# A 128-byte pad that moves the weight tiles of an attention and two-MLP kernel to 256-byte addresses

## The chip, the cores and the metric

One core of a Trainium2 chip runs the whole program. The metric is the device time of one execution in microseconds (us); the median of several executions counts. The profile shows one execution of the same program, recorded instruction by instruction. PE is the matrix engine, PEld its weight load, DVE, ACT and POOL are the other compute engines, and SP issues most of the transfers.

## The reference

```python
# attention: 2 batches, 8 heads, 768 positions, head dimension 64
scores = q @ k.T / 8 + bias          # bias: distance times a slope per head
scores = where(keep, scores, -1e9)   # keep: 8 global keys, 96 local ones
a = exp(scores - max); a = a / (sum(a) + 1e-9)
x = (a @ v) as (1536, 512)
# first block, d_ff 2048
h = x @ w_in;  g = h * sigmoid(h);  x = g @ w_out
# second block, d_ff 1536
g = sigmoid(x @ w_gate) * (x @ w_val);  out = g @ w_out2
```

All inputs and the output are float32 (the weights arrive in a wider layout of two words and are rebuilt on the chip).

## The kernel before

Every large product is done in three passes over pairs of fp32r tiles: each operand is split into a high part and a low part, and hi*hi, hi*lo and lo*hi are added in PSUM. So every activation tile and every weight tile holds two planes: `X[g]` is `[128, 2, 4, 512]` (lines 75, 512), `g` tiles are `[128, 2, 512]` (lines 519 and 533), weight tiles `W[n]` are `[128, 2, 512]` (lines 78 and 920).

The work has two stages. First comes attention with the first half of the first block woven between its steps (`att_units`, `macro`, `window`): there PE alternates between short runs of attention products, PE transposes against `ident`, and fp32r products. Then comes `phase_rest` (line 630), with nothing but fp32r products left for PE: `H(ti)` makes 12 products (24 in the second block) that read an `X` tile and one or two weight tiles into a PSUM bank; `Y(ti)` makes 12 products that read one `g` tile and one weight tile. The order is written out: an `H` run, then the `Y` run of an earlier task, and so on over 68 tasks. Each product of these is 128x128 stationary by 128x512 moving.

- `mm3` (line 501, product on line 503) serves the `H` runs: weight slice stationary, `X` slice moving ("bank<-x,w"). In the attention stage it also serves the output half (`y_part`, line 578): weight slice stationary, `g` slice moving ("bank<-g,w" on L503), in runs of 3 per output slice.
- Line 680 is `Y` of the first block: weight stationary, `g` moving. Line 682 is `Y` of the second: `g` stationary, weight moving.

Weight tiles are filled by `dma_w` (transfer into a `stage` tile), `to_f32` and `split_w` (lines 151 to 168, on ACT and DVE), paced by `pump_w`.

Tiles are laid in the SBUF in the order in which pools and tiles are made. In the program before, byte addresses within a partition are these (they are the compiled program's own):

| tiles | first address | remainder by 256 | by 512 |
|---|---|---|---|
| `ident` | 16512 | 128 | 128 |
| `X[0]`, `X[1]`, `X[2]` | 17152, 33536, 49920 | 0 | 256 |
| `acc[0]`, `acc[1]` | 66304, 74496 | 0 | 256 |
| `nm_all` (384 bytes) | 82688 | 0 | 256 |
| `W[0]` to `W[15]`, every 4096 | 83072 ... | 128 | 128 |
| `stage`, `u`, `g`, `sg` tiles | 148608 ... | 128 | 128 |
| `acc2`, `W[16]` to `W[23]` (made after attention) | 185472, 193664 ... | 128 | 128 |
| attention's `mask`, `kt` | 185472 ... | 128 | 128 |
| attention's `qk`, `v`, `t`, `pt` | 196576 ... | 224 | 480 |

The slices that a product reads start at multiples of 512 bytes within a tile (stationary) or of 1024 (moving), so a slice has its tile's remainder.

Of the kernel before, what the change touches and what calls it, by code (L numbers as in the profile page):

```python
# [8 lines left out]
F32 = mybir.dt.float32  # L9
# [23 lines left out]
def attn_moe_moe2_kernel(  # L33
# [14 lines left out]
    nc = tc.nc  # L48
# [15 lines left out]
    main = fast.enter_context(tc.tile_pool(name="main", bufs=1))  # L64
# [10 lines left out]
    X = [main.tile([128, 2, KD, G], F32R, name=f"x{g}") for g in range(NG)]  # L75
    acc = [main.tile([128, 4, 512], F32, name=f"acc{g}") for g in range(2)]
    nm_all = main.tile([128, NBLK, H], F32, name="nm_all")
    W = [main.tile([128, 2, 512], F32R, name=f"w{n}") for n in range(16)]


# [60 lines left out]
    def wtile(key):  # L141
        return W[wid[key] % 24]

    def slot_free(n):
        if n < 16:
            return True
        if n < 24:
            return len(W) == 24
        return wfree[n - 24] >= 0
# [13 lines left out]
    def split_w(n):  # L163
        w = W[n % 24]
        st = u_p.tile([128, 512], F32, tag="u", name="u")
        to_f32(st, stages.pop(n))
        nc.scalar.activation(out=w[:, 0, :], in_=st, func=AF.Copy)  # L167
        nc.vector.tensor_tensor(w[:, 1, :], st, w[:, 0, :].bitcast(F32), ALU.subtract)  # L168
# [728 lines left out]
    with ExitStack():  # L897
# [21 lines left out]
        for n in range(16, 24):  # L919
            W.append(late.tile([128, 2, 512], F32R, name=f"w{n}"))  # L920
        wst["gap"] = 7
# [38 lines left out]
```

## Time and profile before

| | us |
|---|---|
| median of 3 runs | 691.22 (691.2 to 691.92) |
| the profiled execution, first to last instruction | 690.8 |
| PE busy in it | 676.4 (98%) |
| DVE, ACT, POOL busy | 374.2, 277.5, 84.6 |

The profiled execution's span lies 0.4 us below the median; what lies around the span in a timed run is about that. A matmul's duration in the profile is from its start to its modelled end, with its passage through the pipeline; successive matmuls overlap. So the pace of PE is read from starts: in a merged row of n matmuls, (length of the row minus one matmul's mean duration) / (n - 1) is the mean distance from one start to the next.

### The profile page before, as it was taken

What the parts mean: (1) busy time and instruction counts of PE and PEld (TensorE: products, weight loads), DVE (VectorE), ACT (ScalarE), POOL (GpSimd) and SP (SyncE); (2) the same over time, 40 slices, a digit from 0 to 9 for tenths busy, and PEclk for the clock granted to TensorE, in tenths of its full rate; (3) what the DMA queues carried; (4) which work ended last, traced back from release to release, by engine and by line L of the source; (5) the groups of instructions that cost most, each with busy time, mean ns of one, the idle gap of its engine ahead of it and who ended that gap; (6) DMA issues with size and microseconds to landing.
All of it is one profiled execution on the core that took longest, in us unless ns stands there. A gap on an engine that the chain in (4) does not pass through costs nothing.

```text
span 690.8 us, 9290 instructions
## 1 busy us (share of the span) xinstructions
PE 676.4 (98%) x3463; PEld 539.7 (78%) x3463; DVE 374.2 (54%) x869; ACT 277.5 (40%) x594; POOL 84.6 (12%) x166
## 2 busy tenths in 40 slices
PE   9999999999999999999999999999999999999995
PEld 7567886777778888888888888888888888888884
DVE  4999976534659999452499831211882311212112
ACT  3887865554645555332456521111451111111110
POOL 4255563342410000000000000000000000000000
PEclk9999999999999999999999999999999999999998
DMA  9766652210005554300025420000240000100101
GB/s 212 172 168 170 169 139 62 64 29 3 17 6 155 158 172 136 108 1 0 31 82 169 136 71 1 0 1 0 85 130 0 1 0 1 61 1 23 39 1 65
DMA packets 65301, 49.05 MB, mean 71 GB/s; under 512 B 39648, under 2 KB 60128, under 8 KB 65248
## 3 DMA queue, kind: packets, MB, share of 16 engines
q1 hardware_dynamic: 64032, 48.11, 24.7%
q8 instruction: 29, 0.48, 0.3%
q10 hardware_dynamic: 1216, 0.26, 0.2%
q14 instruction: 24, 0.20, 0.1%
HBM read 45.22 MB, written 3.15 MB: 70 GB/s over the span
## 4 chain that ended last, share of the span: by engine, by line
PE 94%; DVE 4%; issue 1%; ACT 0%; DVEq 0%
PE bank L503 54%; PE bank L682 14%; PE bank L680 13%; PE bank L377 4%; PE bank L449 3%; PE bank L428 2%; PE bank L895 2%; PE bank L340 1%; DVE t L392 1%; DVE acc L589 1%; DVE u L156 0%; DVE w L168 0%; DVE acc L701 0%; DVE ssum L405 0%; DVE u L159 0%
## 5 line engine op out<-in xcount | busy, mean ns | idle before, releaser
L503 PE MATMUL bank<-x,w 128*128 128x512 f32 (+1 forms) x1488 | 354.9, 389 | 0.0
L503 PEld LDWEIGHTS bank<-x,w 128*128 128x128 f32 x1488 | 272.6, 188 | 61.3 <-issue 0.8
L540 DVE TENSOR_TENSOR sg<-sg,bank 128x512 f32<-128x512 f32 x36 | 24.8, 688 | 167.7 <-PE bank L503 167.7
L682 PE MATMUL bank<-w,g 128*128 128x512 f32 x432 | 104.5, 390 | 0.0
L682 PEld LDWEIGHTS bank<-w,g 128*128 128x128 f32 x432 | 81.1, 188 | 17.8
L680 PE MATMUL bank<-g,w 128*128 128x512 f32 x384 | 93.0, 390 | 0.0
L680 PEld LDWEIGHTS bank<-g,w 128*128 128x128 f32 x384 | 72.1, 188 | 16.0
L537 ACT ACTIVATE sg<-bank 128x512 f32<-128x512 f32 x36 | 21.5, 597 | 120.5 <-PE bank L503 120.4
L541 ACT ACTIVATE g<-sg 128x512 fp32r<-128x512 f32 x36 | 22.8, 633 | 93.5 <-DVE sg L540 93.5
L503 PE MATMUL bank<-g,w 128*128 128x512 f32 (+1 forms) x240 | 54.0, 360 | 2.6 <-DVE acc L589 1.3
L154 ACT ACTIVATE u<-stage 128x512 f32<-128x512 f32 x68 | 45.7, 675 | 26.6 <-DVE w L168 26.1
L411 POOL TENSOR_SCALAR t<-t,ssum 128x256 f32<-128x256 f32 (+1 forms) x88 | 48.8, 569 | 61.4 <-DVE ssum L406 23.0
L168 DVE TENSOR_TENSOR w<-u,w 128x512 fp32r<-128x512 f32 x68 | 47.0, 693 | 12.0 <-ACT w L167 11.9
L167 ACT ACTIVATE w<-u 128x512 fp32r<-128x512 f32 x68 | 42.5, 629 | 26.6 <-PE bank L503 10.8
L399 ACT ACTIVATE t<-t,nm_all 128x256 f32<-128x256 f32 (+1 forms) x96 | 46.1, 484 | 17.0 <-DVE nm_all L392 17.0
L159 DVE SCALAR_TENSOR_TENSOR u<-stage,u 128x512 int32<-128x512 int32 x68 | 48.2, 709 | 0.3
L156 DVE SCALAR_TENSOR_TENSOR u<-stage,u 128x512 int32<-128x512 int32 x68 | 46.9, 689 | 0.6
L503 PEld LDWEIGHTS bank<-g,w 128*128 128x128 f32 x240 | 38.0, 189 | 10.6 <-DVE acc L589 3.8
L392 DVE CUSTOM_DVE_ANT_0 t<-bank,mask 128x256 f32<-128x256 f32 (+1 forms) x96 | 33.7, 396 | 17.6 <-PE bank L377 16.7
L528 ACT ACTIVATE g<-sg 128x512 fp32r<-128x512 f32 x48 | 30.3, 631 | 22.4 <-DVE sg L527 11.9
L527 DVE SCALAR_TENSOR_TENSOR sg<-sg,bank 128x512 f32<-128x512 f32 x32 | 21.9, 684 | 30.0 <-ACT sg L526 29.9
L526 ACT ACTIVATE sg<-bank 128x512 f32<-128x512 f32 x32 | 19.1, 596 | 42.9 <-PE bank L503 42.6
(90 smaller groups left out, 515.3 us busy)
## 6 DMA issues: line engine op xcount, KB each, us to landing
stage<-in_moe_w_out_dram SPq DMA_DIRECT2D x28, 512.0 KB, 3.6
stage<-in_moe_w_in_dram SPq DMA_DIRECT2D x16, 512.0 KB, 3.7
stage<-in_moe_w_gate_dram SPq DMA_DIRECT2D x12, 512.0 KB, 3.6
stage<-in_moe_w_val_dram SPq DMA_DIRECT2D x12, 512.0 KB, 3.5
v<-in_v_dram SPq DMA_DIRECT2D x12, 256.0 KB, 3.6
out_dram<-acc SPq DMA_DIRECT2D x12, 256.0 KB, 2.0
qk<-in_k_dram SPq DMA_DIRECT2D x11, 256.0 KB, 3.6
qk<-in_q_dram SPq DMA_DIRECT2D x11, 256.0 KB, 3.9
```

The costliest lines, as they stand in the source:

```text
L154: nc.scalar.activation(out=st, in_=hw.bitcast(F32), func=AF.Copy, scale=2.0 ** -112)
L156: nc.vector.scalar_tensor_tensor(out=ui, in0=lw, scalar=29, in1=ui, op0=ALU.logical_shift_right, op1=ALU.bitwise_or)
L159: nc.vector.scalar_tensor_tensor(out=ui, in0=hw, scalar=-2 ** 31, in1=ui, op0=ALU.bitwise_and, op1=ALU.bitwise_or)
L167: nc.scalar.activation(out=w[:, 0, :], in_=st, func=AF.Copy)
L168: nc.vector.tensor_tensor(w[:, 1, :], st, w[:, 0, :].bitcast(F32), ALU.subtract)
L392: nc.vector.tensor_tensor_reduce(t[:, e, 0:w], sp[e], mask[e][:, m0:m0 + w], op0=ALU.add, op1=ALU.min, scale=-c, scalar=3.0e38, accum_out= ...
L399: nc.scalar.activation(out=t[:, e, 0:w], in_=t[:, e, 0:w], func=AF.Exp, scale=-1.0, bias=nm_all[:, gi, 2 * p + e:2 * p + e + 1], accum_out ...
L411: nc.gpsimd.tensor_scalar(t[:, e, 0:w], t[:, e, 0:w], ss[:, e:e + 1], 1.0, op0=ALU.mult, op1=ALU.mult)
L503: nc.tensor.matmul(ps, wl[(slice(None), a) + wsl], xl[(slice(None), b) + xsl], start=(first and j == 0), stop=(last and j == len(order) - 1),)
L528: nc.scalar.activation(out=gt[:, 0, :], in_=sg, func=AF.Copy)
L680: nc.tensor.matmul(yb[d], w[:, a, sl], gt[:, b, :], start=st, stop=en)
L682: nc.tensor.matmul(yb[d], gt[:, a, sl], w[:, b, :], start=st, stop=en)
```

## The change

A tile of 32 float32 per partition, 128 bytes, is allocated between `nm_all` and `W`, and GpSimd writes zeros into it once. Every tile allocated behind it lies 128 bytes higher: the weight, `stage`, `u`, `g` and `sg` tiles, `acc2` and `mask`/`kt` then have remainder 0 by 256 (256 by 512, as `X` has), and `qk`, `v`, `t`, `pt` have remainder 96 by 256. `ident`, `X`, `acc` and `nm_all` stay.

```diff
     X = [main.tile([128, 2, KD, G], F32R, name=f"x{g}") for g in range(NG)]
     acc = [main.tile([128, 4, 512], F32, name=f"acc{g}") for g in range(2)]
     nm_all = main.tile([128, NBLK, H], F32, name="nm_all")
+    pad = main.tile([128, 32], F32, name="pad")
+    nc.gpsimd.memset(pad, 0.0)
     W = [main.tile([128, 2, 512], F32R, name=f"w{n}") for n in range(16)]
```

## Rows read from the trace of the kernel before

**Rows 1.** Page: span, busy time, granted clock, chain that ended last by engine
```profile
span 690.8 us, 9290 instructions
PE 676.4 (98%) x3463; PEld 539.7 (78%) x3463; DVE 374.2 (54%) x869; ACT 277.5 (40%) x594; POOL 84.6 (12%) x166
PEclk9999999999999999999999999999999999999998
PE 94%; DVE 4%; issue 1%; ACT 0%; DVEq 0%
```

**Rows 2.** Busy time by stretch: length, then each engine (instructions), clock, DMA
```profile
core 0: us, PE busy (x) PEld busy (x) DVE busy (x) ACT busy (x) POOL busy (x), PEclk, DMA share, GB/s
112.00:200.30 88.30, 86.92 (x575) 65.15 (x571) 44.32 (x157) 45.11 (x123) 30.46 (x61) 1.00 0.12 25
200.30:400.00 199.70, 199.70 (x868) 162.68 (x867) 150.71 (x260) 99.02 (x163) 0.00 (x0) 1.00 0.33 102
400.00:682.80 282.80, 282.77 (x1223) 229.18 (x1221) 85.38 (x135) 55.28 (x90) 0.00 (x0) 1.00 0.07 24
```

**Rows 3.** Groups by shape, 200.3 us to end: busy us, mean ns, idle before
```profile
L503 PE MATMUL bank<-x,w 128*128 128x512 f32 x1248 | 302.4, 395 | 0.0
L503 PEld LDWEIGHTS bank<-x,w 128*128 128x128 f32 x1248 | 234.3, 188 | 55.4
L682 PE MATMUL bank<-w,g 128*128 128x512 f32 x432 | 104.5, 390 | 0.0
L680 PE MATMUL bank<-g,w 128*128 128x512 f32 x384 | 93.0, 390 | 0.0
...
L167 ACT ACTIVATE w<-u 128x512 fp32r<-128x512 f32 x52 | 32.5, 630 | 25.1 <-PE bank L503 10.8 <-DVE u L159 8.0 <-PE bank L682 4.0
...
L503 PE MATMUL bank<-g,w 128*128 128x512 f32 x24 | 6.3, 397 | 0.0
```

**Rows 4.** Timeline of PE, end of attention (start us, length us), then the last runs
```profile
199.27 1.09 PE L449 MATMUL bank<-pt,v 128*64 128x128 f32 x16
200.29 1.66 PE L503 MATMUL bank<-g,w 128*128 128x512 f32 x6
201.79 5.73 PE L503 MATMUL bank<-x,w 128*128 128x512 f32 x24
207.36 1.55 PE L503 MATMUL bank<-g,w 128*128 128x512 f32 x6
...
674.43 8.34 PE L682 MATMUL bank<-w,g 128*128 128x512 f32 x36
```

**Rows 5.** Timeline of PE inside the last H run and the last Y run
```profile
664.63 9.96 PE L503 MATMUL bank<-x,w 128*128 128x512 f32 x42
...
676.26 6.51 PE L682 MATMUL bank<-w,g 128*128 128x512 f32 x28
```

**Rows 6.** Chain that ended last, in order of time: start us, length, what
```profile
446.90 5.59 PE bank L503 x24
452.49 2.73 PE bank L682 x12
```

**Rows 7.** Timeline of PE inside runs of 256 moving columns, attention stage
```profile
65.31 1.36 PE L503 MATMUL bank<-g,w 128*128 128x256 f32 x10
...
72.41 2.69 PE L503 MATMUL bank<-x,w 128*128 128x256 f32 x21
```

**Rows 8.** Groups by shape, 0 to 200.3 us, PE
```profile
L503 PE MATMUL bank<-x,w 128*128 128x512 f32 x144 | 37.7, 401 | 0.0
L503 PE MATMUL bank<-g,w 128*128 128x512 f32 x121 | 33.6, 408 | 1.7 <-DVE acc L589 1.3
...
L428 PE MATMUL bank<-ident,t 128*128 128x128 f32 x176 | 28.3, 280 | 0.0
...
L340 PE MATMUL bank<-ident,qk 128*128 128x128 f32 x96 | 20.4, 288 | 1.1 <-ACT kt L353 0.7 <-DVE kt L351 0.4
...
L503 PE MATMUL bank<-x,w 128*128 128x256 f32 x96 | 14.8, 295 | 0.0
L503 PE MATMUL bank<-g,w 128*128 128x256 f32 x96 | 14.7, 292 | 0.9 <-DVE acc L587 0.9
```

**Rows 9.** Timeline of the first 7 us: what GpSimd makes and who needs it
```profile
0.72 0.20 POOL masks.py:197 MEMSET ident<- 128x128 f32 x1 [0.29 <-POOLq L942]
...
1.53 0.29 POOL masks.py:199 TENSOR_SCALAR_AFFINE_SELECT ident<-ident 128x128 f32<-128x128 f32 x1
1.61 0.43 DVE L251 CAST t<-t 128x384 f32<-128x384 int32 x1 [0.62 <-POOL t L249]
...
4.86 0.17 DVE L230 CAST nf<-nraw 128x4 f32<-128x4 int32 x1 [2.82 <-DMA nraw<-in_n_local_dram]
...
6.80 0.27 PE L340 MATMUL bank<-ident,qk 128*128 128x128 f32 x1
```

**Rows 10.** The end of the chain that ended last
```profile
681.45 1.89 DVE acc L701 x3
683.34 0.29 DVEq L925
683.64 0.29 DVE acc L701
```

## The prediction, made before the change was run

> **What bounds the kernel now.** I read the page first, then the busy time by stretch, then single runs of matmuls on PE's timeline. PE is busy for 676.4 of 690.8 us and makes 94% of the chain that ended last, at a granted clock of 0.9 or more in every slice, the last one apart [rows 1]. From 200.3 us on, when attention is over, PE is busy in 199.70 of 199.70 us and then in 282.77 of 282.80 us at a clock of 1.00 [rows 2], and no matmul group there has any idle time before it [rows 3]. DVE is busy for 150.71 us of the first of these stretches and 85.38 us of the second [rows 2], and a step of the weight preparation (L167) waits for PE, not PE for it [rows 3]. So in the last 482 us only one thing can change the time: the distance from one matmul's start to the next.
>
> **The pace of PE there.** The stage holds 1248 + 432 + 384 + 24 = 2088 products of 512 columns [rows 3]. The first starts at 200.29, the last ends at 674.43 + 8.34 = 682.77 [rows 4]; without the last one's own 0.39 us that is 482.09 us for 2087 distances, 231.0 ns each. But the distances are not alike. Inside the last H run (L503, X moving, weight stationary) it is (9.96 - 0.395) / 41 = 233.3 ns; inside the last Y run (L682) it is (6.51 - 0.39) / 27 = 226.7 ns [rows 3, 5]. Both are 128x128 by 128x512 at the same clock, with one weight load for each product, with nothing to wait for. In the middle of the stage it is the same: an H piece of the chain takes 5.59 / 24 = 232.9 ns each, a Y piece 2.73 / 12 = 227.5 [rows 6]. (A Y run comes in a little slower and then settles: 12 x 227.5 = 2730, less nine at 226.7, leaves 230 ns for each of its first three.) The last Y run goes over three tasks, thus over three pairs of weight and g tiles, and L682 has g stationary and the weight moving while L680 has it the other way round; both groups have the same mean of 390 ns against 395 for L503 [rows 3]. So neither a new tile nor the roles of the tiles make the difference.
>
> What does differ is where the operands start. In Y both start at remainder 128 by 512. In H the weight slice starts at 128 and the X slice at 256. The start of the slice within a tile can't matter much: H steps through four slices of each weight plane and of each X plane, and the mean stays. I take this as the reason: the load of the next product's weights (188 ns, with no time of its own on PE's path [rows 3]) reads the SBUF while the present product streams its moving operand, and the two lie better or worse to each other by the distance of their start addresses.
>
> **The change part by part.**
> *The addresses.* X stays at 256 by 512; weight and g tiles go from 128 to 256. H gets the distance 0 that Y has now; Y keeps its distance of 0. If distance alone decides, each of the 2087 distances becomes 226.7 ns, those at the entrance of a Y run too, since there is no other pace to come from: 2087 x 226.7 = 473.1 us in place of 482.1, a gain of 9.0 us. About 1248 x (232.8 - 226.7) = 7.6 us of it comes from H, the rest from the first products of Y runs and from 24 products of L503 on g. If the entrance of Y stays as it is, the gain is 7.6: that is the lower bound of this case.
>
> *The attention stage.* The 144 products of X there have a mean of 401 ns, the 121 on g, whose operands are at distance 0 already, 408 [rows 8]. They come in short runs between attention's work; six on g take (1.55 - 0.397) / 5 = 230.6 ns each, and the 24 on X beside them (5.73 - 0.395) / 23 = 232.0 [rows 4]. Runs too short to settle gain little, so I count nothing there; the upper bound is some 200 products by 5 ns, 1.0 us. Products of 256 columns show next to no difference: (2.69 - 0.295) / 20 = 119.8 ns on X, (1.36 - 0.292) / 9 = 118.7 on g [rows 7, 8]. I count nothing for them. PE's transposes read `ident` (which stays at 128) and tiles that go from 224 to 96. No row shows that pair of remainders. Bounded by the nearest effect, 6.6 ns either way on 176 + 96 transposes [rows 8], that is 1.8 us up or down; I take 0, since their distance is no more a multiple of 256 after than before.
>
> *The memset.* The nearest row is the memset of `ident` on the same engine, 0.20 us for four times the columns [rows 9]. It may push GpSimd's first work back by up to that. What covers it: `ident` is ready at 1.82 us and PE first uses it at 6.80; the positions that DVE casts at 1.61 us are followed by a wait of 2.82 us for a transfer [rows 9]. Cost 0; without that cover, 0.2 us. GpSimd does nothing after 200.3 us [rows 2]. The order of instructions comes from a planner that simulates times, so one instruction more can exchange neighbours elsewhere in attention: I leave 0.3 us either way for that.
>
> *The others.* ACT's and DVE's operands move by 128 bytes too. They are not on the path before the last evacuation; the tail is three additions of 1.89 us together, one more of 0.29, and the last transfer [rows 10]; I count no change.
>
> Sum: 690.8 - 9.0 = 681.8 us of span, and with the 0.4 us between span and median 691.2 - 9.0 = 682.2. What is late next is still PE: with 231.0 going to 226.7 it asks for weights 2% earlier, and DVE, at 150.71 of 199.70 us, has a quarter to spare.
>
> **The rivals.**
> *It doesn't matter (691.2 us).* The cause could be something else in which H differs from Y: X's two planes lie 8 KiB apart, those of g and W 2 KiB, and H steps to a new X slice every three products. For it: the trace has no run of 512 columns on X at distance 0. Against it: Y's pace didn't change when it stepped to other tiles. The price is that of the whole effect, so the time stays. [...]
>
> *A moving operand at remainder 0 by 256 is itself the slow one (695 us).* H's moving operand starts there and is slow, Y's starts at 128 and is fast [rows 5]; the trace can't tell that from distance, since it has only these two pairs. Then H stays as it is, and all 816 Y products and the 24 on g take H's 232.8 ns in place of 228.1 on average: 840 x 4.7 = 3.9 us more, 695.1. The place is lines 680 and 682; it decides as soon as a settled Y run goes over 230 ns. Against it: a cost of a single stream's start should show as well at 256 columns, where it is within 1.1 ns [rows 7], though there the weight load of 188 ns [rows 3] may hide either cause.
>
> **How the numbers follow.** Forecast (distance decides): 0.64. No effect: 0.19. Slower by the moving start or by the unknown pairs: 0.17. Predicted time 682.2. Its own range is 680.6 (attention gains its 1.0 us, planner 0.3, transposes a little) to 685.5 (entrance of Y runs stays, 1.4, and 1.8 us lost on transposes). The whole range must take in the case of no effect, with the 0.4 us by which the slowest run of before stands off: 680.5 to 691.9. A measurement of this kernel tells about 0.2% (1.4 us) from no change; by that, faster 0.64, same 0.19, slower 0.17.
>
> **What would show it.** Right: in the last H run 42 matmuls in 0.395 + 41 x 0.2267 = 9.69 us in place of 9.96, H pieces of the chain at 5.44 us for 24, the mean of L503 on X in the last stage at 390 ns, Y groups still at 390 or just under, and the attention stage's end within 0.5 us of 200.3. The second rival would show as Y pieces of 2.8 us for 12. No effect would show as 9.96 again. I am wrong if the pace goes to a third value on all groups, or if transposes change by more than 6 ns each.

## The result and the profile after

The kernel with the pad takes 681.88 us (median of 4 runs, 681.57 to 682.99) against 691.57 us (4 runs, 691.20 to 692.33). The ratio on record is 0.9866, with a 95% interval of 0.9852 to 0.988; the quotient of the two medians is 0.9860. The forecast was 682.2. Over all runs of the kernel before that were taken beside the experiments, 19 of them, its median is 691.26. Line numbers of the kernel after are larger by 2.

The page of the kernel after, the lines that answer to [rows 1] (PEclk is the granted clock in 40 slices of the span, in tenths):

```profile
span 680.0 us, 9291 instructions
PE 667.6 (98%) x3463; PEld 540.1 (79%) x3463; DVE 374.2 (55%) x869; ACT 277.9 (41%) x594; POOL 84.6 (12%) x167
PEclk9899999999999999999999999999999999999999
PE 93%; DVE 5%; ACT 1%; issue 0%; DVEq 0%
```

PE's busy time is 8.8 us less; that of no other engine has changed by more than 0.4 us. The 8 in the clock's row lies in the attention stage: from 27 to 34 us the granted clock was 0.76 on average, and from 29 to 32 us it was 0.50; the trace before has 1.00 from 27 to 34 us. PE had been busy for 12.00 of the 12 us ahead of it, as in the trace before. The last stage doesn't see it. Busy time by stretch (length, then each engine with its instructions, granted clock, DMA share, GB/s), as in [rows 2]:

```profile
112.00:199.60 87.60, 86.22 (x570) 64.99 (x568) 44.06 (x155) 45.09 (x123) 30.07 (x60) 1.00 0.11 24
199.60:400.00 200.40, 200.40 (x886) 165.94 (x885) 152.40 (x263) 100.49 (x164) 0.00 (x0) 1.00 0.34 105
400.00:672.90 272.90, 272.90 (x1206) 225.88 (x1204) 83.11 (x131) 54.37 (x88) 0.00 (x0) 1.00 0.07 22
```

PE has no gap in the last stage, as before, and the clock is 1.00 as before; in about the same 200 us it makes 886 products in place of 868. So the pace is what changed. The groups by shape from 199 us on (busy us, mean ns, idle before), to be read beside [rows 3]:

```profile
L505 PE MATMUL bank<-x,w 128*128 128x512 f32 x1248 | 294.7, 389 | 0.0
L505 PEld LDWEIGHTS bank<-x,w 128*128 128x128 f32 x1248 | 234.2, 188 | 48.6
L684 PE MATMUL bank<-w,g 128*128 128x512 f32 x432 | 103.9, 389 | 0.0
L682 PE MATMUL bank<-g,w 128*128 128x512 f32 x384 | 92.4, 389 | 0.0
```

The products on X have lost their 395 ns and stand at 389 with the others; the weight load's 188 ns is what it was. The timeline of PE (start us, length us) gives the stage's two ends, and the insides of the last H run and the last Y run, for [rows 4] and [rows 5]:

```profile
199.61 1.66 PE L505 MATMUL bank<-g,w 128*128 128x512 f32 x6
...
664.87 8.32 PE L684 MATMUL bank<-w,g 128*128 128x512 f32 x36
```

```profile
655.80 8.55 PE L505 MATMUL bank<-x,w 128*128 128x512 f32 x37
...
666.68 6.51 PE L684 MATMUL bank<-w,g 128*128 128x512 f32 x28
```

H: (8.55 - 0.389) / 36 = 226.7 ns, where it was 233.3. Y: 6.51 us for 28, to the digit what it was. The stage lasts from 199.61 to 664.87 + 8.32 = 673.19, 473.58 us in place of 482.48: 8.9 us less. In the chain that ended last (start us, length, what), where [rows 6] had 5.59 and 2.73:

```profile
441.99 5.44 PE bank L505 x24
447.43 2.72 PE bank L684 x12
```

12 x 226.7 = 2.72: the slow entrance of the Y runs is gone too. Taken over all starts in the trace, the distance is 226.67 ns on average for the 1248 products on X, for L682 and for L684 alike; on X it was 232.8 and for L680 and L682 of the kernel before 228.2 and 228.0.

The span fell by 10.8 us, 1.9 more than the stage. That rest isn't the change's. 0.7 us of it lies ahead of 200 us, where the first product on loaded data starts 0.9 us earlier (6.80 us in [rows 9]):

```profile
5.91 0.27 PE L342 MATMUL bank<-ident,qk 128*128 128x128 f32 x1
```

In the experiments below it starts between 5.5 and 7.0 us, with no relation to the pads. The other 1.2 us lie behind the last product: 8.0 us from its end to the span's end before, 6.8 after. In experiment 1 below, which has the same pace, that stretch is 8.2 us; it varies by itself. The timed difference from the 691.26 of the 19 runs, 9.4 us, has less of it.

### The profile page after: what moved, and what is told of

Its sections match the earlier page's. It is cut to its first block, busy times and chain, and to the rows that moved or that the text cites. A ratio compares the mean times of both kernels' runs of the same rounds, so it can differ in the third digit from the quotient of the medians.

```text
span 680.0 us, 9291 instructions
## 1 busy us (share of the span) xinstructions
PE 667.6 (98%) x3463; PEld 540.1 (79%) x3463; DVE 374.2 (55%) x869; ACT 277.9 (41%) x594; POOL 84.6 (12%) x167
## 4 chain that ended last, share of the span: by engine, by line
PE 93%; DVE 5%; ACT 1%; issue 0%; DVEq 0%
PE bank L505 54%; PE bank L684 14%; PE bank L682 13%; PE bank L379 4%; PE bank L451 3%; PE bank L430 2%; PE bank L897 2%; PE bank L342 1%; DVE t L394 1%; DVE acc L591 1%; DVE w L170 0%; DVE u L158 0%; DVE u L161 0%; DVE acc L703 0%; ACT t L401 0%
## 5 line engine op out<-in xcount | busy, mean ns | idle before, releaser
L505 PE MATMUL bank<-x,w 128*128 128x512 f32 (+1 forms) x1488 | 347.1, 384 | 0.0
L684 PE MATMUL bank<-w,g 128*128 128x512 f32 x432 | 103.9, 389 | 0.0
L684 PEld LDWEIGHTS bank<-w,g 128*128 128x128 f32 x432 | 81.1, 188 | 16.8
L682 PE MATMUL bank<-g,w 128*128 128x512 f32 x384 | 92.4, 389 | 0.0
L682 PEld LDWEIGHTS bank<-g,w 128*128 128x128 f32 x384 | 72.1, 188 | 15.0
```

Source lines behind the costliest of these rows:

```text
L505: nc.tensor.matmul(ps, wl[(slice(None), a) + wsl], xl[(slice(None), b) + xsl], start=(first and j == 0), stop=(last and j == len(order) - 1),)
L682: nc.tensor.matmul(yb[d], w[:, a, sl], gt[:, b, :], start=st, stop=en)
L684: nc.tensor.matmul(yb[d], gt[:, a, sl], w[:, b, :], start=st, stop=en)
```

## The experiments

**1. Nothing at a multiple of 256, all at the same remainder.** Was it the aligned start or the distance of zero?

```diff
+    padx = main.tile([128, 32], F32, name="padx")
+    nc.gpsimd.memset(padx, 0.0)
     X = [main.tile([128, 2, KD, G], F32R, name=f"x{g}") for g in range(NG)]
...
+    pad = main.tile([128, 32], F32, name="pad")
+    nc.gpsimd.memset(pad, 0.0)
     W = [main.tile([128, 2, 512], F32R, name=f"w{n}") for n in range(16)]
```

> A pad of 128 bytes ahead of X and another of 128 bytes ahead of W: X, W, g and all between lie at remainder 128 by 256, none of them at a multiple of 256, and the distance between moving and stationary start is 0 in all 2088 products of the last stage. Theory (the distance decides): the same as with the change, 681.9 us, every distance from start to start in the last stage 226.7 ns. Rival (X and its weights have to start at multiples of 256 bytes themselves): H runs stay slow, 691 us or, if Y suffers too, 695.

Measured: 682.45 us, ratio 0.9871 (0.9853 to 0.9889), as with the change. The chain that ended last has the same pieces:

```profile
441.04 5.44 PE bank L507 x24
446.48 2.72 PE bank L686 x12
```

So no operand needs a multiple of 256. X at remainder 128 is as fast as X at 0 once its weights lie at 128 as well: from its first to its last start the last stage took 473.19 us in both kernels.

**2. The g tiles and a third of the weights off.** If the distance decides, Y must become slow where its operands differ, on tiles on which it was fast before.

```diff
+    pad = main.tile([128, 32], F32, name="pad")
+    nc.gpsimd.memset(pad, 0.0)
     W = [main.tile([128, 2, 512], F32R, name=f"w{n}") for n in range(16)]
+    padg = main.tile([128, 32], F32, name="padg")
+    nc.gpsimd.memset(padg, 0.0)
```

> The change with a second pad of 128 bytes behind W[15]: X and W[0] to W[15] lie at remainder 0 by 256, the g tiles and W[16] to W[23] (allocated after attention) at 128. In the last stage 852 products of H are then at distance 0 and 396 at 128, of Y 324 at 0 and 516 at 128. Theory (the distance decides, whichever operand is off): 912 products at about 233 ns, thus 912 x 6.3 = 5.7 us above the change, 687.6 us; Y runs on W[0] to W[15] at 233 ns, where in the kernel before they were at 226.7 on the same tiles. Rival (only X is sensitive, by its layout or by its start): Y runs stay at 226.7 ns everywhere and the time is 681.9 + 396 x 6.3 = 684.4 us.

Measured: 689.8 us, ratio 0.9974 (0.9963 to 0.9986). The pieces of the chain, each on one side of the line:

```profile
601.25 2.80 PE bank L686 x12
604.05 5.48 PE bank L507 x24
...
620.59 5.58 PE bank L507 x24
626.17 2.78 PE bank L686 x12
```

At 601.25 and 604.05 the weights lie at 0: the Y run, whose g lies at 128, takes 2.80 / 12 = 233 ns each, which no settled Y run did before, and the H run takes 5.48 / 24 = 228. At 620.59 the weights are W[16] and later, at 128: H takes 5.58 / 24 = 232.5. So the same X tile is fast or slow by the weight tile that it meets, and Y is sensitive as H is. (The Y run at 626.17, with g and weights both at 128, is at distance 0 and still takes 2.78 us: it comes from a slow H run, and by its starts it settles only with its tenth product.) The theory's time was too low by 2.2 us, and the rival's by 5.4. What the theory's sum left out are the entrances: the products at distance 0 have a mean of 228.1 ns there (all starts in the trace), not 226.7, since each run has to settle anew. 1176 of them by 1.5 ns are 1.7 us; with 912 x 6.2 = 5.7 that makes 7.4. The last stage took 7.3 us longer than with the change, from the start of attention's last product to the last start (480.7 us against 473.4).

**3. A pad of 256 bytes.** The same instructions as the change, but the distance in H back at half of 256.

```diff
+    pad = main.tile([128, 64], F32, name="pad")
+    nc.gpsimd.memset(pad, 0.0)
     W = [main.tile([128, 2, 512], F32R, name=f"w{n}") for n in range(16)]
```

> A pad of 256 bytes in place of 128, with its memset: X at 256 by 512, W and g at 384 by 512, so the distance in H is 128 by 256 again, with the other sign by 512. Theory (distance by 256): as before, 691.2 to 691.6 us, H at 233 ns, Y at 226.7. Rival (distance by 512, or the larger address of W alone): H goes to a third pace, and the time off 691 by more than 1.4 us. Second rival (the memset and the shift of the planner's order gave part of the gain): under 690.5.

Measured: 691.59 us, ratio 1.0003 (0.9993 to 1.0012): the kernel before, in the chain's pieces as well.

```profile
445.88 5.59 PE bank L505 x24
451.47 2.73 PE bank L684 x12
```

From first to last start the last stage took 482.09 us, as before. The added instruction and the shift of all that lies behind bring nothing; the distance by 256 does.

**4. The pad without its memset.**

```diff
+    pad = main.tile([128, 32], F32, name="pad")
     W = [main.tile([128, 2, 512], F32R, name=f"w{n}") for n in range(16)]
```

> The change with the pad allocated and never written. Theory: the memset is hidden and the addresses do everything, 681.9 us within 0.3. Rival (the instruction more on GpSimd moves something in the first stage by 0.2 us or more, in either way): off 681.9 by 0.2 to 0.7 us, with the end of attention at another time than in the change.

Measured: 682.75 us, ratio 0.987 (0.9852 to 0.9887). Its four runs go from 682.39 to 682.95, those of the change from 681.57 to 682.99, so no part of the gain that could be told from scatter is the memset's. From first to last start the last stage took 473.19 us with the memset and without it, and the memset's own 0.12 us on GpSimd don't show. A difference of 0.3 us can't be told from scatter: the median is 0.87 us above that of the change and 0.3 above that of experiment 1, which has two memsets. The expected "within 0.3" was narrower than that scatter, and so was the 0.7 of its rival; by these bounds alone the run speaks for neither.

**5 to 7. The pace at other distances.** One kernel has three X tiles, so it can hold three distances at once: pads ahead of each of them (32 bytes each in the first kernel; 160, 32 and 32 in the second), and one ahead of W that brings it back to a multiple of 256.

```diff
-    X = [main.tile([128, 2, KD, G], F32R, name=f"x{g}") for g in range(NG)]
+    X = []
+    padx0 = main.tile([128, 8], F32, name="padx0")
+    nc.gpsimd.memset(padx0, 0.0)
+    X.append(main.tile([128, 2, KD, G], F32R, name="x0"))
...
+    pad = main.tile([128, 8], F32, name="pad")
+    nc.gpsimd.memset(pad, 0.0)
     W = [main.tile([128, 2, 512], F32R, name=f"w{n}") for n in range(16)]
```

> W and g at remainder 0 by 256 as with the change, and small pads ahead of each X tile, so that X[0], X[1] and X[2] start 32, 64 and 96 bytes behind a multiple of 256. Y stays at distance 0. The pace of H is read for each X tile apart, from starts. Theory A (two paces: any distance but 0 costs the same): 232 to 233 ns for all three, about 691 us. Theory B (graded: the stretch grows with the distance up to the 6.2 ns at 128): some 228, 230 and 231.5 ns, about 686 us. Theory C (chunks of 64 bytes: 64 is as good as 0): 32 and 96 slow, 64 at 226.7.

> The same with X[0], X[1] and X[2] at 160, 192 and 224 bytes behind a multiple of 256 (W and g at 0 by 256). Theory A: 232 to 233 ns for all three. Theory B, if only the size of the distance counts: 224 as 32, 192 as 64, 160 as 96. If the order counts (the stream ahead of the weights or behind them), the two sides differ.

In the third kernel X[0] is moved by 256 bytes, and X[1] and X[2] are views that begin 4 and 2 elements into a larger tile.

```diff
-    X = [main.tile([128, 2, KD, G], F32R, name=f"x{g}") for g in range(NG)]
+    X = []
...
+    for g, off in ((1, 4), (2, 2)):
+        xw = main.tile([128, 2 * KD * G + 128], F32R, name=f"x{g}")
+        X.append(xw[:, off:off + 2 * KD * G].rearrange("p (a k f) -> p a k f", a=2, k=KD))
```

> W and g at 256 by 512; X[0] at 0 by 512, thus at distance 0 by 256 but 256 by 512; X[1] and X[2] 16 and 8 bytes off a distance of 0. Theory (the pattern repeats every 256 bytes): X[0] at 226.7 ns. Rival (it repeats every 512 bytes or more): X[0] slower. For 16 and 8 bytes: theory A 232 to 233 ns, theory B 227 to 227.5, hardly to be told from 226.7.

Measured, one run each: 692.38, 694.09 and 690.29 us. A piece of the chain for each X tile, of 24 products. Distances 32, 64 and 96:

```profile
530.90 5.60 PE bank L514 x24
...
581.06 5.51 PE bank L514 x24
...
630.74 5.61 PE bank L514 x24
```

Distances 160, 192 and 224:

```profile
531.03 5.62 PE bank L514 x24
...
581.11 5.60 PE bank L514 x24
...
631.15 5.60 PE bank L514 x24
```

Distances 256, 16 and 8:

```profile
528.53 5.44 PE bank L513 x24
...
577.49 5.56 PE bank L513 x24
...
627.33 5.60 PE bank L513 x24
```

Over all starts of the last stage the mean distances are:

| bytes between the starts, by 256 | ns from start to start |
|---|---|
| 0 (both at the same remainder) | 226.7 |
| 0 (256 by 512) | 226.7 |
| 8 | 233.3 |
| 16 | 231.5 |
| 32 | 233.4 |
| 64 | 229.8 |
| 96 | 234.1 |
| 128 (kernel before) | 232.8 |
| 160 | 234.0 |
| 192 | 233.3 |
| 224 | 233.5 |

Theory A comes nearest: eight of the nine distances between 0 and 256 cost 4.9 to 7.4 ns, as much at 8 bytes as at 128. In these three kernels only X was moved, so at these distances a cost of the distance and a cost of X's own start can't be told apart; experiments 1 and 2 do that for 128 alone. The graded theory B falls, with its forecast of 227 to 227.5 ns for 8 and 16 bytes. Theory C is half right at 64, which costs 3.1 ns, and wrong in its mirror, as 192 costs 6.7. The pattern repeats after 256 bytes at both places where that was tried: X[0] at 256 by 512 has the full pace, and 384 by 512 (experiment 3) costs what 128 by 512 costs in the kernel before, 232.8 ns. The kernel before took 691.72 us beside them, but single runs spread by more than these differences, so the last stage from first to last start tells more: 483.4, 483.2 and 479.3 us, against 482.1 in the kernel before. In the first, H is no slower on average than before (232.5 ns), but the Y runs behind it settle later (230 ns on average against 228.1); in the second H is slower (233.6); in the third one X tile has the full pace. No distance gave a pace under 226.7, so there is no version here that beats the change.

**8. Which load does a product suffer from?** Only the low plane of each g tile is put off by 128 bytes (the edit of `act1` is shown; `act2` has the same).

```diff
+    pad = main.tile([128, 32], F32, name="pad")
+    nc.gpsimd.memset(pad, 0.0)
...
-        gt = g_p.tile([128, 2, 512], F32R, tag="g", name="g")
+        gt = g_p.tile([128, 2, 544], F32R, tag="g", name="g")[:, :, 0:512]
```

> The change, with 128 bytes more between the high and the low plane of each g tile, so that only the low plane of g lies at 128 by 256 and all else at 0. In the second block's Y runs (g stationary) products go in threes: g high with W high, g high with W low, g low with W high. The load of the low plane is made for the third product and runs while the second streams. Theory (a product is stretched by the load that runs under it, which is that of the next product): by place in the three, the second one's distance to the next start is longer than the two others'. Rival (a product is stretched by its own weights' start): the third one's is longest. In the first block's Y runs (g moving) the low plane streams second, and the second product is the slow one in both. H stays at 226.7 ns where it doesn't follow Y. Time: 560 products of Y can stay at 227 to 229, 280 go up by 6 ns or more: some 684 to 686 us.

Measured: 684.9 us, one run, inside what was expected. The groups from 199 us on:

```profile
L505 PE MATMUL bank<-x,w 128*128 128x512 f32 x1248 | 294.8, 389 | 0.0
L684 PE MATMUL bank<-w,g 128*128 128x512 f32 x432 | 105.9, 394 | 0.0
L682 PE MATMUL bank<-g,w 128*128 128x512 f32 x384 | 93.2, 391 | 0.0
```

H stays at 389, and both kinds of Y have grown, L684 (g stationary) by more. By place in the three, over all starts: on L682, where the low plane streams second, 226.7, 234.1 and 225.9 ns; on L684, where it is the third product's weights, 227.0, 232.4 and 234.1 ns. So on L684 neither theory holds alone: the second product, under which the off weights are loaded, is stretched, and so is the third, which uses them. One off load costs two products, one off stream one. The time came out inside the expected range although that counted one slow product in three on L684, and there are two. Whether the third product is long by its own weights' start, or only settles behind the second as the entrances do in experiment 2, these runs don't show; it stays open.

## Why the prediction was right

**The bound.** Right: in the last stage PE's distance from start to start was all there was to gain, and it stays the bound at 226.7 ns. Weights were never late: no group of products has idle time before it in the last stage (0.0 us each).

**The term of the sum.** Predicted 9.0 us, measured 8.9 in the traces. 7.7 of them come from products on X (1248 x (232.8 - 226.67)), where 7.6 was forecast, and 1.1 from the entrances of Y runs, which the forecast took from one argument: that the slow first three products came from the H run ahead of them. Experiment 2 bears that out from the other side, since the entrances came back with the runs at distance 128. That the median lies within 0.3 us of the forecast is closer than such medians repeat: three kernels with this same pace have 681.88, 682.45 and 682.75 us. The last tenths are luck. The whole range, 680.5 to 691.9, took in the case of no effect, so that the time lies in it says little; the paces that it named (H pieces of 5.44 us, a mean of 390 ns where 389 was measured) say more. (Its upper end is the slowest run of before, which stands 0.7 us off the median there and not 0.4.)

**The reason.** The forecast's distance holds, by experiments 1, 2 and 3. That the load of the next weights lies in the time of the present product is in the traces: in the last stage nearly every load starts 3 or 4 ns behind a product's start and takes 188 ns, before and after. That the two lie better or worse to each other was the author's guess and remains one: the runs show that the loss goes with the distance between the two starts (232.8 ns at 128, 226.7 at 0), and that a product at distance 0 can take 232.4 ns when the weights loaded meanwhile are off (experiment 8); by what means, no run shows. The expectation that a small distance costs little was wrong, but the sum didn't rest on it.

**The rivals.** "It doesn't matter" fell with the result. A distance of 128 bytes in place of 0 costs 6.2 ns for each product on X (232.8 against 226.7), and in experiment 8 a product whose own two operands lie at 0 is stretched to 232.4 ns while the off weights of the next are loaded under it. So here a product's time depends on the start of the weights that are loaded under it, too. "A moving operand at 0 is itself slow" fell too: the moving operand of every product starts at 0 now. The argument against it from runs of 256 columns was weak: their mean durations, 295 and 292 ns [rows 8], are the same after the change, in the groups ahead of 199.6 us:

```profile
L505 PE MATMUL bank<-x,w 128*128 128x256 f32 x96 | 14.9, 295 | 0.0
L505 PE MATMUL bank<-g,w 128*128 128x256 f32 x96 | 14.7, 292 | 0.9 <-DVE acc L589 0.9
```

On X they are 295 ns at a distance of 128 and at 0, so they couldn't speak for either cause.

**What was counted at nothing.** The attention stage: from the first product on loaded data to the last of attention 193.3 us before and 193.5 after, so no gain and no loss that can be told from scatter (the other traces have 192.9 to 193.8), though the distances of its few settled products on X did fall (230.2 from 231.8 ns in 115 of them, which is 0.2 us). The end of attention, which was to stay within 0.5 us of 200.3, came at 199.6, by the earlier first product; that sign was narrower than the scatter (198.7 to 200.4 over the experiments). The transposes against `ident`, with the new pair of remainders: two of them on `t` that follow each other directly start 109 ns apart (median), before and after. Their mean durations did rise, by 5 and 7 ns against [rows 8], where the forecast had called more than 6 ns a sign of being wrong:

```profile
L430 PE MATMUL bank<-ident,t 128*128 128x128 f32 x176 | 29.0, 285 | 0.0
...
L342 PE MATMUL bank<-ident,qk 128*128 128x128 f32 x96 | 20.9, 295 | 0.7 <-ACT kt L355 0.7
```

The addresses are not the reason: in experiment 4, which has those of the change, the means are 280 and 288 as before. Of the ten traces just the three with a stretch at a lower granted clock between 28 and 33 us (this one, at 0.50 from 29 to 32 us, and those of experiments 5 and 8; over their whole spans the three have 0.995, the others 0.996 to 0.999) have longer means. In this one the seven transposes on `t` and the five on `qk` that start between 28.5 and 32.1 us last 398 and 402 ns on average, the others 280 and 289. The memset: hidden (experiment 4). The 0.4 us between span and median is not what lies around the span in a timed run: every run on record that has a span of its own was timed 1.7 to 1.9 us above it, that of the kernel after at 681.75 with a span of 680.0. The 0.4 came from setting the span of one execution beside the median of others. The sum went from median to median, and so didn't suffer from that.

## What to carry to other kernels

Where PE is the bound and loads new weights for every product, read the distance from start to start of each kind of matmul apart; two kinds of the same shape with different paces are a reason to look at where their operands start. Let the moving and the stationary operand of fp32r products of 512 columns start at the same remainder by 256 bytes (here 226.7 ns from start to start, against 229.8 to 234.1 at the other distances tried), and check that no small tile allocated between them breaks it: here a table of 384 bytes cost 1.3% of the kernel. Which common remainder it is made no difference between 0 and 128, the two that were tried.

## What the runs showed of the hardware that was not expected

- With X moved, eight bytes between the starts cost as much as 128 (233.3 against 232.8 ns); of nine distances other than 0 by 256 only 64 was clearly cheaper (229.8).
- At the same remainder the pace is the same for every product, 226 or 227 ns from start to start for all but a handful of the last stage's 2087; in the settled H runs of the kernel before, at 128, it alternates, 229 or 230 and 237 or 238, though the operands repeat only every three products.
- A run at distance 0 behind one at another distance needs two to ten products until its pace settles (experiments 2, 5 and 7).
- One weight plane off goes with two slow products, 232.4 and 234.1 ns, one moving plane off with a single one, 234.1 (experiment 8).
